# Three-chunk value visits, transposed cluster scores and a re-planned order in a clustered-attention and mixture kernel

## The chip, the cores and the metric

The kernel runs on one core of a Trainium2 chip, as one launch. The metric is the device time of a launch in microseconds. The core has five engines that run their own instruction queues in order: TensorE (PE in the profile; its weight loads PEld), VectorE (DVE), ScalarE (ACT), GpSimd (POOL) and SyncE (SP), whose queue issues most transfers. Results of TensorE land in PSUM; everything else lives in SBUF.

## The reference

Sixteen heads of attention (2 batches x 8 heads, 768 positions, head size 64) in which a query sees only the keys whose nearest centroid is its own, then a soft mixture of eight experts with four slots each, then a gated layer. Cut to what matters:

```python
q_assign = argmax(einsum('bhsd,hcd->bhsc', q_n, c_n))   # 16 clusters
k_assign = argmax(einsum('bhsd,hcd->bhsc', k_n, c_n))
scores = where(q_assign == k_assign, scale * q @ k.T, -1e9)
attn = softmax(scores) @ v
x = attn.transpose(0, 2, 1, 3).reshape(B * S, H * D)
logits = x @ phi                                        # 8 experts x 4 slots
slot_input = softmax(logits, axis=0).T @ x
slot_out[e] = relu(slot_input[e] @ w1[e]) @ w2[e]
x = softmax(logits, axis=1) @ slot_out
xn = x / sqrt(mean(x * x) + 1e-6) * rms_g
out = (silu(xn @ w_gate) * (xn @ w_val)) @ w_out
```

## The kernel before

Heads are taken two at a time: eight pairs, numbered i. `prepare(i)` loads q, k and v of a pair, splits every value into a high and a low part (`tokq`, `tokk`; the low part is a subtraction on GpSimd or VectorE), turns the result with TensorE (`ptk`, `ptq`, L331) and copies it out of PSUM (`k1`, `q1`). It does so in two halves g of 384 positions. Per half it then forms the centroid scores of q and k (`pc`, L368), copies them to SBUF (`cs`), brings them back to one position per partition by products against a constant `G2` that adds the two partial sums (`sc`, L378), finds the winning cluster with five VectorE steps (`am`, `E`, L399 to L408) and turns the one-hot rows `E` with TensorE (`pe`, L419). ScalarE writes them into the extra rows of `q2` and `k2` (`oq`, `ok`), so that the score products also carry the mask.

A unit u is one half of the queries of a pair: 16 units. Each first computes raw scores (`s1`, L489) whose row maxima VectorE takes (`nm`, L501), turns the maxima (`pm`, L519) and moves them into a row of `q2` with a transfer (`mrow`). Then six key chunks c follow: the scores again, with mask and maximum (`s2`, L541 and L543, four passes), the exponential on ScalarE (`P`, L550), the sum of the P tiles on GpSimd (`acc`, L217) and the value products (`o`, L567), which use 64 of the 128 columns of the array, one head in each half. `AVN = 2` makes one visit to the value products for every two chunks, so three visits per unit. `RINGS` gives the number of buffers of each kind; P has `PR = 5`, and PSUM gives three buffers to `big` (s1, s2, transposes, row sums) and one each to `ms` (`pc`, `sc`, `pe`, `pm`, `po`) and `av` (`o`).

Nothing of the order is written out by hand. Every step is an `op` with its possible engines and their estimated durations, its inputs, the buffers that it takes and a key, the time at which it is due in units; `KO` shifts the key of a kind of step. `Sched.run` lists the steps one after the other: it takes the one that could start first by the estimates, plus a penalty for a later key (`WK`), and thereby fixes each engine's queue.

The weights of the last layer arrive as 64-bit words and are decoded beside attention: 24 tiles into `wgv`, two into `wo4`, each with a step on ScalarE (`mag`) and two on VectorE (`bits`, L914 and L916). The experts' weights, 64 loads of 512 KB, go into 31 places that are freed one after another (`xa` to `xc`, `rawk` to `tokq`, rings `w0`, `wx`, `wz`, `wv`, `wy`); the last four rings open when parts of the attention buffers are closed. After attention come the slot sums (`middle`), the experts (`h1`, `h2`), and the gated layer in three groups of tokens (`g`, `v`, `hf`, `hh`, `hl`, `o`, L1614).

Of the kernel before, what the change touches and what calls it, by code (L numbers as in the profile page):

```python
# [7 lines left out]
F32 = mybir.dt.float32  # L8
# [9 lines left out]
C = 16  # L18
# [9 lines left out]
def bc(ap, n):  # L28
# [16 lines left out]
WK = 6.8
# [13 lines left out]
DK = 1.74  # L59
# [7 lines left out]
PT = 219.23  # L67
# [44 lines left out]
class Sched:  # L112
# [7 lines left out]
    LAT = dict(pe=200, act=150, dve=130, pool=80)  # L120
# [21 lines left out]
    def run(self):  # L142
# [9 lines left out]
        done = 0  # L152
        while avail:
            best = None
            k0 = min(o.key for o in avail)
            for o in avail:
# [24 lines left out]
            free[e] = st + busy  # L181
            o.end = st + dur
# [41 lines left out]
class Attention:  # L224
# [7 lines left out]
    def __init__(self, tc, sched, K, q, k, v, X, pools, cw):  # L232
# [7 lines left out]
        self.lastE = []  # L240
        self.final = {}
# [35 lines left out]
    def prepare(self, i):  # L277
# [22 lines left out]
        def half(g):  # L300
# [44 lines left out]
            for n, nm in enumerate("kq"):  # L345
# [5 lines left out]
                l = op({"pool": (1020, 1020, 0 if i else P0), "dve": 550}, split_lo(nm), key=zg - 14.5, uses=[(a, t), (O[r], r)])  # L351
                p = op({"pe": 550}, trans(nm), key=zg - 12 + 0.4 * n, alloc=("big", nm + "1", nm + "2"),
# [1470 lines left out]
```

## Time and profile before

| | |
|---|---|
| median of 3 runs | 500.8 us (500.64 to 501.13) |
| the profiled execution | 499.88 us, of which the span of the trace 497.8 us |
| TensorE busy | 467.3 us (94%), 2872 instructions |
| VectorE, ScalarE, GpSimd busy | 318.1 us, 283.8 us, 191.2 us |
| read from HBM | 61.97 MB |

The profile gives the busy time of every engine, the time of every instruction and what it waited for. The stages stand one after another in the span: opening to 30 us, attention to 297.4, slot sums to 310, experts to 361, the start of the gated layer to 376.4, its products to 491.5 and the last output to 497.8. A busy time is that of the whole stretch asked for; the granted clock is TensorE's, 1.00 for 2.4 GHz.

### The profile page before, as it was taken

Reading aid. Unit: us, or ns where it says so; the run is one execution under the profiler, and the core shown is the slowest. Engines: PE = TensorE matmul, PEld = TensorE weight load, DVE = VectorE, ACT = ScalarE, POOL = GpSimd, SP = SyncE. Lnnn points to the kernel's source line nnn. Section 1 sums busy time; section 2 is a strip of 40 time slices with the busy share of each in tenths; the row PEclk is TensorE's granted clock in tenths of the full one; section 3 lists DMA queues with packets and bytes.
Section 4 is the critical chain, followed back from the end, with each engine's and each line's share of the span. In section 5 each row is a group of like instructions: output and inputs, shape, how many; then the busy total and the mean of one; then the engine's idle time right before and its main releaser. Section 6 shows DMA issues by size and latency. Waiting matters only on the chain.

```text
span 497.8 us, 7957 instructions
## 1 busy us (share of the span) xinstructions
PE 467.3 (94%) x2872; PEld 328.1 (66%) x2872; DVE 318.1 (64%) x607; ACT 283.8 (57%) x586; POOL 191.2 (38%) x130
## 2 busy tenths in 40 slices
PE   7899998999999999999999997989899999999996
PEld 6766676675766856765765774335347888888884
DVE  6879998989999999765738236100169884443430
ACT  5687686696795876865551653220248665335331
POOL 2237745666574656655464650100214550000000
PEclk9999999999999999999998998999999999999999
DMA  6564633634634541203922974899922302002002
GB/s 182 155 197 116 197 122 95 169 113 124 182 114 110 172 133 48 65 17 105 349 91 85 348 257 158 343 390 403 394 78 86 127 1 84 2 0 86 0 0 84
DMA packets 30822, 71.96 MB, mean 145 GB/s; under 512 B 4064, under 2 KB 10304, under 8 KB 30784
## 3 DMA queue, kind: packets, MB, share of 16 engines
q1 hardware_dynamic: 26080, 55.73, 33.3%
q10 hardware_dynamic: 4704, 15.73, 10.1%
q8 instruction: 22, 0.36, 0.3%
q14 instruction: 16, 0.13, 0.1%
HBM read 61.97 MB, written 3.15 MB: 131 GB/s over the span
## 4 chain that ended last, share of the span: by engine, by line
PE 73%; DVE 14%; DMA 6%; ACT 3%; issue 2%; ACTq 0%; POOL 0%; SPq 0%; DVEq 0%
PE o L1614 20%; PE o L567 11%; PE s L541 8%; PE s L543 6%; DVE nm L501 5%; PE s L489 5%; DMA w<-in_moe_w_dram 4%; PE h L1297 2%; PE pc L368 2%; DVE wgv L916 2%; PE h L1271 2%; PE g L1578 2%; PE v L1578 2%; PE pl L598 2%; PE sc L378 1%
## 5 line engine op out<-in xcount | busy, mean ns | idle before, releaser
L217 POOL TENSOR_TENSOR acc<-acc,P 128x768 f32<-128x768 f32 x62 | 115.3, 1860 | 49.5 <-ACT P L550 47.2
L550 ACT ACTIVATE P<-s 128x768 f32<-128x768 f32 x96 | 76.1, 812 | 45.7 <-PE s L543 43.8
L501 DVE TENSOR_REDUCE nm<-s 128x1 f32<-128x768 f32 x96 | 88.5, 950 | 19.6 <-PE s L489 18.7
L1614 PE MATMUL o<-W,hh 128*128 128x512 f32 x288 | 89.6, 392 | 0.0
L541 PE MATMUL s<-q,k 128*128 128x384 f32 x192 | 72.2, 376 | 3.4 <-DVE nm L501 2.8
L567 PE MATMUL o<-P,rawv 128*64 128x384 f32 x384 | 72.1, 498 | 0.0
L543 PE MATMUL s<-q,k 97*128 97x384 f32 x192 | 65.4, 341 | 0.9 <-DMA q<-nr 0.9
L1614 PEld LDWEIGHTS o<-W,hh 128*128 128x128 f32 x288 | 53.9, 188 | 12.2
L1614 PE MATMUL o<-W,hl 128*128 128x512 f32 x144 | 56.7, 394 | 0.0
L489 PE MATMUL s<-k,q 96*128 96x384 f32 x192 | 51.7, 370 | 1.4 <-DVE nm L501 1.3
L217 POOL TENSOR_TENSOR acc<-P,P 128x768 f32<-128x768 f32 x16 | 29.6, 1849 | 56.2 <-ACT P L550 56.2
L541 PEld LDWEIGHTS s<-q,k 128*128 128x128 f32 x192 | 36.5, 190 | 18.7 <-DVE nm L501 8.3
L1590 DVE TENSOR_TENSOR hf<-v,sg 128x512 f32<-128x512 f32 x36 | 24.6, 689 | 33.6 <-PE v L1578 30.1
L567 PEld LDWEIGHTS o<-P,rawv 128*64 128x64 f32 x384 | 23.5, 136 | 28.1 <-issue 26.8
L489 PEld LDWEIGHTS s<-k,q 96*128 96x128 f32 x192 | 32.0, 193 | 11.8 <-DVE nm L501 5.5
L543 PEld LDWEIGHTS s<-q,k 97*128 97x128 f32 x192 | 36.8, 192 | 1.2 <-DMA q<-nr 1.2
L217 POOL TENSOR_TENSOR W<-wo,W 128x512 fp32r<-128x512 f32 x10 | 13.9, 1389 | 58.8 <-DMA w<-in_moe_w_dram 35.9
L1586 ACT ACTIVATE sg<-g 128x512 f32<-128x512 f32 x36 | 21.3, 598 | 24.9 <-PE g L1578 24.7
L209 ACT CAST hh<-hf 128x512 fp32r<-128x512 f32 x34 | 21.1, 621 | 22.1 <-PE o L1614 21.0
L217 DVE TENSOR_TENSOR hl<-hf,hh 128x512 fp32r<-128x512 f32 x32 | 24.5, 766 | 13.0 <-ACT hh L209 12.3
L1614 PEld LDWEIGHTS o<-W,hl 128*128 128x128 f32 x144 | 27.0, 188 | 6.1
L623 ACT ACTIVATE pl<-pl 128x128 f32<-128x128 f32 x84 | 22.0, 262 | 8.3 <-PE pl L605 4.6
(250 smaller groups left out, 740.0 us busy)
## 6 DMA issues: line engine op xcount, KB each, us to landing
w<-in_moe_w_dram SPq DMA_DIRECT2D x56, 512.0 KB, 7.3
gate<-in_moe_w_gate_dram ACTq DMA_DIRECT2D x12, 512.0 KB, 3.5
val<-in_moe_w_val_dram ACTq DMA_DIRECT2D x12, 512.0 KB
out<-in_moe_w_out_dram SPq DMA_DIRECT2D x10, 512.0 KB, 4.9
rawk<-in_k_dram SPq DMA_DIRECT2D x8, 384.0 KB, 3.6
rawq<-in_q_dram SPq DMA_DIRECT2D x8, 384.0 KB, 3.8
rawv<-in_v_dram SPq DMA_DIRECT2D x8, 384.0 KB, 4.7
k<-k SPq DMA_DIRECT2D x16, 192.0 KB, 3.1
```

The source lines that it names most:

```text
L209: nc.scalar.copy(out, in_)
L217: (nc.vector if e == "dve" else nc.gpsimd).tensor_tensor(out, a, b, op=op)
L489: nc.tensor.matmul(ps[:, g, :HQ], T[q2][0:96, h, qb : qb + 128], T[f"k2_{i}_{g}"][0:96, h, :], start=True, stop=True,)
L501: nc.vector.tensor_reduce(T[f"nm{u}"][:, n : n + 1], T[f"s1_{u}{h}{j}"][:, :, :HQ], op=ALU.max, axis=AX.XY, negate=True)
L541: nc.tensor.matmul(ps[:, h, :HQ], T[f"k1_{i}_{g}"][:, h, kb], T[q1][:, h, :], start=True, stop=False)
L543: nc.tensor.matmul(ps[:, h, :HQ], T[f"k2_{i}_{g}"][0:97, h, kb], T[q2][0:97, h, :], start=False, stop=True)
L550: nc.scalar.activation(p, T[f"s2_{u}_{c}"][:, :, :HQ], AF.Exp, scale=float(1.0 / D**0.5))
L567: nc.tensor.matmul(T[f"o{u}"][64 * h : 64 * h + 64, :HQ], T[f"rawv{i}"][:, h, c, :], T[f"P{u}_{c}"][:, h, :], start=(c == 0), stop=(c == N ...
L623: nc.scalar.activation(p, p, AF.Copy, accum_out=ls_()[:, h, j : j + 1])
L1586: nc.scalar.activation(self.tile(f"sg{tg}_{f}", [128, 512], F32, "sg", "outp", 2), T[f"g{tg}_{f}"], AF.Silu)
L1590: nc.vector.tensor_tensor(self.tile(f"hf{tg}_{f}", [128, 512], F32, "hf", "outp", 2), T[f"v{tg}_{f}"], T[f"sg{tg}_{f}"], op=ALU.mult)
L1614: nc.tensor.matmul(T[f"o{tg}{q}"], T[f"{x}{tg}_{f}"][:, ts], T[f"W{f // 6}"][:, w, f % 6, :], start=(f == 0 and n == 0), stop=(f == 11 and ...
```

## The change

The value products are made in two visits of three chunks (`AVN = 3`), and P has seven buffers. The cluster scores are turned by three transposes against the identity instead of products with `G2`; the two partial sums that the product added are added by a new VectorE step `part` with two reductions. The one-hot rows of q and k lie side by side in a tile 96 wide, so that three transposes bring all of them (`E` is written in another layout, and `oq` and `ok` read the new place); the constants `escale` and `ebias` move with them, and `G2` goes. The planner charges TensorE for going into and out of the value products and for starting after a gap, has other durations, other delays between engines, two new order constraints (`lastT`) and new numbers in its tables. The ring `wx` has six places instead of eight, `wv` and `wy` five instead of four each.

```diff
-PR = 5
+PR = 7
-AVN = 2
+AVN = 3
-NW0, NWX, NWZ, NWV, NW1 = 4, 8, 4, 4, 4
+NW0, NWX, NWZ, NWV, NW1 = 4, 6, 4, 5, 5
...
 KO = {
-    "oT": -6.7, "s1": 0.19, "lT": -0.03, "split_hi": 17.5, "osb": -15.77, "mag": 8.64, "guard": 7.48, "argmax": -16.77,
+    "oT": -7.28, "s1": -0.53, "lT": 1.63, "split_hi": 87.73, "osb": -14.23, "mag": 11.6, "guard": 7.48,
+    "argmax": -7.55, "oevac": 15.28, "clusterT": 3.91, "lsum": 0.75, "onehot": -2.04, "acc": -35.81, "av": 33.0,
...
-    LAT = dict(pe=200, act=150, dve=130, pool=80)
+    LAT = dict(pe=180, act=140, dve=100, pool=80)
+
+    HALF = ("av",)
+    TO, FRO, COLD = 140, 200, 100
...
+        def more(o, e, st):
+            if e != "pe" or o.key > 99:
+                return 0
+            h = opname(o.fn) in self.HALF
+            return (self.TO if h else self.FRO) if h != half else 0 if h or st < free.get(e, 0.0) + 5 else self.COLD
+
...
-                l = op({"pool": (1020, 1020, 0 if i else P0), "dve": 550}, split_lo(nm), key=zg - 14.5, uses=[(a, t), (O[r], r)])
+                l = op({"pool": (1250, 1250, 0 if i else P0), "dve": (850, 850, SLP if i else 0)}, split_lo(nm), key=zg - 14.5, uses=[(a, t), (O[r], r)])
...
                 for j in range(3):
-                    nc.tensor.matmul(pt[:, 64 * j : 64 * j + 64], T[f"cs{i}{g}"][:, j * 128 : (j + 1) * 128], K["G2"],
-                                     start=True, stop=True)
+                    at = slice(j * 128, (j + 1) * 128)
+                    nc.tensor.transpose(pt[:, 128 + j * 128 :][:, :128], T[f"cs{i}{g}"][:, at], K["id"])
+
+
+            def part(e):
+                pt = T[f"sc{i}{g}"]
+                for a, b in ((0, 128), (128, 192)):
+                    nc.vector.tensor_reduce(pt[:, a:b].rearrange("p (m c) -> p m c", c=C),
+                                            pt[:, 128 + 2 * a : 128 + 2 * b].rearrange("p (m t c) -> p m c t", t=2, c=C),
+                                            op=ALU.add, axis=AX.X)
...
+            self.lastT = [p]
+            p = op({"dve": 640}, part, key=zg - 9.9, uses=[SC])
...
-                            self.tile("E", [128, 3, 65], BF16, "E")
-                            nc.vector.memset(T["E"][:, :, 64:], 1.0)
+                            self.tile("E", [128, 3, 96], BF16, "E")
+                            nc.vector.memset(T["E"][:, :, 32:64], 1.0)
...
                 pt = self.bank(f"pe{i}{g}", ms).bitcast(BF16)
-                for n in range(2):
-                    for j in range(3):
-                        at = n * HQ + j * 128
-                        nc.tensor.transpose(pt[64:97, at : at + 128], T["E"][:, j, 32 * n : 32 * n + 33], K["idb"])
+                for j in range(3):
+                    nc.tensor.transpose(pt[:96, j * 128 : (j + 1) * 128], T["E"][:, j], K["idb"])
...
-                pv.append(op({"pe": 650 * AVN + 170}, av(cs), key=zu + c + 1.3, alloc=() if pv else ("av",),
+                pv.append(op({"pe": 646 * AVN + 10}, av(cs), key=zu + c + 1.3, alloc=() if pv else ("av",),
```

Three places in the queues show what the tables do. TensorE, in the middle of attention: units 6 (`o6`, `s2_6`) and 7, the second half of pair 4 (`sc41`, `pe41`); "..." stands for the second head's two passes of the same score step. Before:

```order
L378 MATMUL sc41_1726<-G2_132,cs41_1682 128x64 x3
L598 MATMUL pl5_1735<-idr_102,acc5_1519 128x128 x6
L605 MATMUL pl5_1735<-phi_99,os5_1671 128x64 x3
L541 MATMUL s2_6_3_1751<-q1_3_0_1034,k1_3_1_1238 128x384
L543 MATMUL s2_6_3_1751<-q2_3_0_1035,k2_3_1_1239 128x384
...
L567 MATMUL o6_1764<-P6_0_1689,rawv3_1304 64x384 x2
L567 MATMUL o6_1764<-P6_1_1724,rawv3_1304 64x384 x2
L419 LDWEIGHTS E_296
L419 MATMUL pe41_1776<-idb_104,E_296 33x128
```

And now, the same place:

```order
L403 MATMUL sc41_1721<-idr_102,cs41_1692 128x128 x3
L355 MATMUL ptq50_1735<-idr_102,tokq5_0_1588 128x128 x6
L601 MATMUL o6_1745<-P6_0_1612,rawv3_1280 64x384 x2
L601 MATMUL o6_1745<-P6_1_1651,rawv3_1280 64x384 x2
L601 MATMUL o6_1745<-P6_2_1676,rawv3_1280 64x384 x2
L575 MATMUL s2_7_0_1767<-q1_3_1_1159,k1_3_0_1053 128x384
L577 MATMUL s2_7_0_1767<-q2_3_1_1160,k2_3_0_1054 128x384
...
L453 LDWEIGHTS E_302
L453 MATMUL pe41_1776<-idb_104,E_302 96x128
```

The visit takes three chunks, and the row sums of unit 5 (`pl5`) have moved ahead of `sc41`. VectorE at the same place, the steps that make the one-hot rows (`wgv` is a weight decode, `nr7` and `l5` belong to units 7 and 5). Before:

```order
L501 TENSOR_REDUCE nm7_1599<-s1_712_1712 128x1
L916 SCALAR_TENSOR_TENSOR wgv_151<-val1_3_1454,daval1_3_1616 128x512
L399 TENSOR_REDUCE am41_1745<-sc41_1726 128x12
L401 TENSOR_TENSOR sc41_1726<-sc41_1726,am41_1745 128x192
L404 SCALAR_TENSOR_TENSOR sc41_1726<-sc41_1726,iota_113 128x192
L406 TENSOR_REDUCE am41_1745<-sc41_1726 128x12
L408 TENSOR_TENSOR E_296<-sc41_1726,am41_1745 128x3x64
```

And now:

```order
L945 SCALAR_TENSOR_TENSOR wgv_150<-gate1_1_1416,dagate1_1_1674 128x512
L409 TENSOR_REDUCE sc41_1721<-sc41_1721 128x128
L409 TENSOR_REDUCE sc41_1721<-sc41_1721 128x64
L433 TENSOR_REDUCE am41_1752<-sc41_1721 128x12
L435 TENSOR_TENSOR sc41_1721<-sc41_1721,am41_1752 128x192
L668 TENSOR_SCALAR pl5_1706<-pl5_1706 128x6
L438 SCALAR_TENSOR_TENSOR sc41_1721<-sc41_1721,iota_113 128x192
L670 RECIPROCAL l5_1758<-pl5_1706 128x6
L440 TENSOR_REDUCE am41_1752<-sc41_1721 128x12
L442 TENSOR_TENSOR E_302<-sc41_1721,am41_1752 128x3x2x32
```

The two reductions come in, two small steps of unit 5 stand between, and the decode ahead is an earlier one (`gate1_1` for `val1_3`): decodes now run to unit 14, where they ended in unit 10. SyncE near the end of attention: `nr13` to `nr15` are the maxima of the last units, the `w` loads are expert weights. Before:

```order
L204 DMA q2_6_1_2427<-nr13_2940 1x6x128
L204 DMA q2_7_0_2595<-nr14_3103 1x6x128
L880 DMA w21_2_3128<-in_moe_w2_dram 128x2x512
L880 DMA w20_1_3143<-in_moe_w2_dram 128x2x512
L880 DMA w20_3_3153<-in_moe_w2_dram 128x2x512
L880 DMA w21_1_3165<-in_moe_w2_dram 128x2x512
L880 DMA w21_3_3189<-in_moe_w2_dram 128x2x512
L880 DMA w12_0_3205<-in_moe_w1_dram 128x1024
L204 DMA q2_7_1_2797<-nr15_3191 1x6x128
L880 DMA w13_0_3215<-in_moe_w1_dram 128x1024
```

And now:

```order
L227 DMA q2_6_1_2357<-nr13_2891 1x6x128
L227 DMA q2_7_0_2543<-nr14_3057 1x6x128
L227 DMA q2_7_1_2746<-nr15_3169 1x6x128
L909 DMA w21_2_3187<-in_moe_w2_dram 128x2x512
L909 DMA w20_1_3208<-in_moe_w2_dram 128x2x512
```

The six loads that stood ahead of unit 15's maxima stand behind them.

## Rows read from the trace of the kernel before

**Rows 1.** Busy times by stretch: us; PE, PEld, DVE, ACT, POOL; clock, DMA share, GB/s
```profile
30.00:297.40 267.40, 255.78 (x1565) 179.66 (x1564) 209.07 (x379) 184.37 (x401) 157.16 (x89) 0.99 0.46 145
88.00:192.10 104.10, 100.41 (x625) 71.31 (x625) 95.93 (x171) 79.26 (x179) 63.55 (x36) 1.00 0.46 134
268.40:272.40 4.00, 4.00 (x15) 3.33 (x14) 2.86 (x4) 1.12 (x3) 2.65 (x2) 0.57 0.35 131
297.40:310.00 12.60, 8.92 (x85) 6.03 (x82) 6.80 (x25) 4.96 (x20) 0.00 (x0) 0.86 0.55 198
310.00:361.00 51.00, 47.47 (x417) 19.87 (x417) 5.55 (x17) 10.42 (x20) 4.39 (x10) 1.00 0.98 374
376.40:491.50 115.10, 115.10 (x506) 93.80 (x505) 63.01 (x86) 56.88 (x99) 17.39 (x12) 1.00 0.12 42
```

**Rows 2.** TensorE's waits in attention (us, times, longest), and one in time
```profile
PE s L541 <- DVE nm L501: 2.8, 7, 0.7
PE pc L368 <- DVE k L211: 2.5, 4, 0.7
...
264.85 0.62 PE L489 MATMUL s<-k,q 96*128 96x384 f32 x2 [0.34 <-DVE nm L501]
```

**Rows 3.** TensorE in time (start, us): around one value visit, and a double one
```profile
142.02 0.34 PE L541 MATMUL s<-q,k 128*128 128x384 f32 x1
142.20 0.34 PE L543 MATMUL s<-q,k 97*128 97x384 f32 x1
142.46 1.51 PE L567 MATMUL o<-P,rawv 128*64 128x384 f32 x8
143.90 0.44 PE L541 MATMUL s<-q,k 128*128 128x384 f32 x1
144.18 0.34 PE L543 MATMUL s<-q,k 97*128 97x384 f32 x1
...
292.91 2.80 PE L567 MATMUL o<-P,rawv 128*64 128x384 f32 x16
```

**Rows 4.** TensorE in time: one-hot rows, three transposes, cluster scores, with followers
```profile
134.10 0.51 PE L419 MATMUL pe<-idb,E 128*33 128x128 bf16 x6
134.54 0.62 PE L489 MATMUL s<-k,q 96*128 96x384 f32 x2
...
160.46 0.55 PE L628 MATMUL po<-idr,os 128*128 128x128 f32 x3
160.76 0.42 PE L541 MATMUL s<-q,k 128*128 128x384 f32 x1
...
161.91 0.78 PE L378 MATMUL sc<-G,cs 128*128 128x64 f32 x6
162.50 0.59 PE L489 MATMUL s<-k,q 96*128 96x384 f32 x2
```

**Rows 5.** VectorE's groups, 88 to 192.1 us (the last: whole run): busy us, mean ns
```profile
L501 DVE TENSOR_REDUCE nm<-s 128x1 f32<-128x768 f32 x36 | 33.5, 951 | 4.8 <-PE s L489 4.4
L916 DVE SCALAR_TENSOR_TENSOR wgv<-gate,dagate 128x512 int32<-128x512 int32 x8 | 10.4, 1298 | 0.0
L914 DVE TENSOR_SCALAR dagate<-dagate 128x512 int32<-128x512 int32 x8 | 9.9, 1251 | 0.0
L211 DVE CAST k<-ptk 128x768 fp32r<-128x768 f32 x4 | 3.8, 944 | 0.0
L217 DVE TENSOR_TENSOR tokq<-rawq,tokq 128x384 fp32r<-128x384 f32 x3 | 3.4, 1141 | 0.0
L401 DVE TENSOR_TENSOR sc<-sc,am 128x192 f32<-128x192 f32 x6 | 2.2, 361 | 0.3
...
L673 DVE TENSOR_REDUCE L<-pl 128x64 f32<-128x128 f32 x4 | 1.1, 284 | 0.1
```

**Rows 6.** SyncE's queue in time (start, us)
```profile
269.73 3.01 SPq L880 DMA_DIRECT2D w<-in_moe_w_dram  x6
...
279.27 63.62 SPq L880 DMA_DIRECT2D w<-in_moe_w_dram  x43
```

More of the change, by code (lines that the diff above doesn't have):

```diff
@@ L30, in bc @@
     return ap.unsqueeze(len(ap.shape)).to_broadcast(list(ap.shape) + [n])
-SH = 8.49
-SH1 = 2.63
+SH = 9.28
+SH1 = 2.66
 DMAT = 2400.0
 DMAB = 600.0
-SHP = 11.22
-SHQ = 2.9
+SHP = 20.84
+SHQ = 1.84
 SLK = 2000.0
 NKQ = 4
-DG = 2.05
-LP = 753.69
-DP = 301.31
-PR = 5
-WK = 6.8
+DG = 3.0
+LP = 18052.37
+DP = 232.12
+PR = 7
+WK = 7.76
 WKT = 200.0
@@ L66 @@
 WC = 500.0
-PT = 219.23
+WM = 0.3
+SLP = 477.95
+PT = 478.56
 OA = 2
@@ new lines @@
+LGP = 61.14
+AVN = 3
+LP = 18052.37
+AP = 13381.6
+GP = 6842.73
+XP = 9896.11
+NW0, NWX, NWZ, NWV, NW1 = 4, 6, 4, 5, 5
+KO = {
+    "oT": -7.28, "s1": -0.53, "lT": 1.63, "split_hi": 87.73, "osb": -14.23, "mag": 11.6, "guard": 7.48,
+    "argmax": -7.55, "oevac": 15.28, "clusterT": 3.91, "lsum": 0.75, "onehot": -2.04, "acc": -35.81, "av": 33.0,
+    "evac": 0.88, "bits": -1.18, "nmT": -13.35, "split_lo": -42.25, "s1max": -8.76, "cevac": 5.66, "nrow": 21.47,
+    "cluster": 2.34, "csum": -9.29, "lga": -22.47, "lgm": 69.26, "hh": 58.86, "pre": -0.68, "rms0": -0.9, "h2e": -6.42,
+    "part": -3.71, "low": -39.37, "soh": 0.05, "hl": 17.17, "gh": -6.79, "cTe": -49.34, "raw": -10.52, "om": 1.29,
+    "cT": -3.78, "sot": -2.04, "lo": 43.74, "gcols": -64.55, "put4": 26.77, "x2s": -1.21, "gp": 51.24, "hi": 9.62,
+    "silu": -18.04, "x2": -66.93, "rows": 0.57, "siT": -12.69, "si": -40.13, "dz": 3.33, "mx": -17.5, "mp": 28.55,
+    "dexp": 52.02, "sie": -25.75, "cq": -18.95, "qhi": -20.63, "fexp": -29.39, "gram": 0.46, "socs": -103.61,
+    "fold": 23.44, "fsi": 46.62, "fz": -35.81, "qlo": -7.16, "drec": -53.26, "mv": -38.65, "linv": -26.33,
+    "xrow": -11.36, "exp": 6.89, "trans": -1.86, "mrow": -23.15, "oq": -16.8, "sums": 3.0, "tok": 8.0, "ok": 10.96,
+    "centroids_": 25.86, "cols": -11.58, "csm": -43.42, "ds": 5.45, "dsum": -45.11, "fes": -34.61, "four": 0.49,
+    "h1": 87.53, "h2": -3.34, "hT": -9.72, "hTe": 8.9, "hf": 47.46, "high": -17.99, "lgt": 24.63, "lgx": -82.97,
+    "lgx0": 21.44, "load": 65.08, "mb": 42.7, "mm": -0.66, "mp1": -28.22, "mpT": 3.01, "od": -42.59, "oe": 10.74,
+    "put": -3.64, "relu": 62.21, "rms": -79.22, "root": 30.84, "s2": -1.24, "scale": -8.08, "sel": 42.33,
+    "setup": -61.3, "siT0": 6.25, "siTe": 5.35, "side": 44.61, "siz": -5.05, "square": -4.15, "to_out": -53.23,
+    "to_tail": 48.79, "to_wp": -24.39, "to_wv": -26.44, "to_wx": 13.35, "to_wz": 14.8, "warm": 19.04, "wload": -10.88,
@@ L152, in run @@
         done = 0
+        half = False
+        def more(o, e, st):
[3 more added lines that the diff above has]
+            return (self.TO if h else self.FRO) if h != half else 0 if h or st < free.get(e, 0.0) + 5 else self.COLD
         while avail:
@@ L173, in run @@
                     pen = d[2] if isinstance(d, tuple) and len(d) > 2 else 0
+                    pen += WM * more(o, e, st)
                     pen += min((WK if o.key < 99 else WKT) * (o.key - k0), WC)
@@ L180, in run @@
             busy, dur = d[:2] if isinstance(d, tuple) else (d, d)
-            free[e] = st + busy
-            o.end = st + dur
+            x = more(o, e, st)
+            if e == "pe" and o.key <= 99:
+                half = opname(o.fn) in self.HALF
+            free[e] = st + busy + x
+            o.end = st + dur + x
             o.seen = o.end + self.LAT.get(e, 0)
@@ L509, in unit @@
                 key = zu - 5.5 + 0.66 * n - sh
-                p = op({"pe": 420}, s1(h, j), key=key,
+                p = op({"pe": 360}, s1(h, j), key=key,
                        deps=O["q2r", half] + O["k2r", 0] + O["k2r", 1] + ([U[0]] if n else []),
@@ L574, in unit @@
             d = md + O["q2r", half] + O["k2r", c // 3]
-            s = op({"pe": 760}, s2(c), key=zu + c, deps=d, alloc=("big",),
+            s = op({"pe": 715}, s2(c), key=zu + c, deps=d, alloc=("big",),
                    uses=[K1[c // 3], K2[c // 3], Q1, Q2])
@@ L920, in decode @@
         a = op({"act": (670, 670, pen)}, mag, key=key, deps=deps, after=[self.prev[0]], uses=[src], alloc=("da",))
-        b = op({"dve": (600, 600, pen)}, bits(0), key=key + 0.01, uses=[(a, "da")])
-        d = op({"dve": (1050, 1050, pen)}, bits(1), key=key + 0.02, deps=[b], after=[self.prev[1]], alloc=alloc,
+        b = op({"dve": (920, 920, pen)}, bits(0), key=key + 0.01, uses=[(a, "da")])
+        d = op({"dve": (1270, 1270, pen)}, bits(1), key=key + 0.02, deps=[b], after=[self.prev[1]], alloc=alloc,
                uses=[src, (a, "da")])
```

53 lines of the change are left out of this document (21 added, 32 removed), and 3 rows, old and new, of the table KO.

## The prediction

> **What bounds the kernel now.** I cut the span into stages first [rows 1] and asked of each who ends it. In the attention stretch from 30 to 297.4 us TensorE is busy for 255.78 of 267.4 us, VectorE for 209.07, so TensorE sets the pace with 11.6 us of gaps. In the three steady pairs of units from 88 to 192.1 us (34.7 us each) the two stand closer together: TensorE 100.41, VectorE 95.93 of 104.1, which is 92% for VectorE. From 310 to 361 us, the experts, the DMA share is 0.98: this stage ends when the last expert weight has landed, whatever TensorE could do. From 376.4 to 491.5 us TensorE has no gap at all, and the change takes no multiplication out of that stage. The end of the attention stretch is therefore what can move, and the later stages follow it as a block if the experts' transfers keep their distance to it.
>
> Next I read what TensorE waits for inside the stretch [rows 2]. The largest two are the row maxima (`nm`, L501) and the copy of the transposed keys out of PSUM (`k`, L211), both on VectorE; 2.5 us hang on the latter, in four waits. To the gaps comes a slow piece: from 268.4 to 272.4 us TensorE is busy throughout at a mean granted clock of 0.57, so mostly at 1.2, the lower of the two levels (2.4 GHz is the other), after score products (`s1`) that had waited one by one for a maximum [rows 2]. At full clock that work takes 4.0 x 0.57 = 2.3 us, so 1.7 us are lost. Gaps and clock together are 13.3 us, the most that a better order could give back in attention.
>
> **The value products, 46 visits to 30.** A visit to the half-width products (`o`, L567) costs more than its passes. In [rows 3] the last score pass starts at 142.20, the second one after the visit at 144.18; passes of the scores start 0.18 us apart, so the visit occupies 144.00 - 142.38 = 1.62 us. Its eight passes are worth 1.29 us: that is the difference between the entry with 16 passes (2.80) and the one with eight (1.51). The remaining 0.33 us is paid per visit, for going in, draining and coming out. The old order has 46 visits (two of the 48 stand back to back with another), the new order 30, counted in the listings. 16 x 0.33 = 5.3 us of TensorE. The bounds are 0, if the cost sits in the passes, and 5.3.
>
> **Cluster scores turned by transposes.** Six passes against `G2` start at 161.91 and the next work at 162.50, 0.59 us [rows 4]. Three transposes of the same kind of data (`po`, L628) take from 160.46 to 160.76, 0.30 us, and the work behind either starts up alike. I take 0.30 for the new step, so 0.29 x 16 = 4.6 us; if each new transpose cost as much as two old passes, nothing would be gained, so the bounds are 0 and 4.6.
>
> **One transpose for the one-hot rows.** Six products took 134.10 to 134.54 = 0.44 us [rows 4]. Half as many, 96 columns wide instead of 33, should take 0.22; the bounds are 0.22 and 0.44, since nothing in the trace shows that width here. I take 0.22, because the row is for the same 128 columns that pass in each; 0.22 x 16 = 3.5 us. The three parts together are 13.4 us of TensorE, 1.7 us per pair.
>
> **What VectorE pays.** The two cluster hypotheses now are added by two reductions per half, of 256 and of 128 values per partition. The nearest rows are a reduction of 128 values, 284 ns, and of 768 values, 951 ns [rows 5]: in between, 256 values take about 0.42 us, so 0.70 us per half and 1.4 per pair. Against that, in a steady pair: the `k` copy leaves VectorE (0.94 us), both subtractions for `tokq` and `tokk` leave it in most pairs (1.14 for the one in the row; I count 1.7 for both), and the 26 weight decodes, about five per pair in this stretch (eight of its 15 are in the row), are spread over units 2 to 14, some four per pair: one less, 1.30 + 1.25 = 2.6 us. The pair needs 95.93/3 = 32.0 + 1.4 - 0.9 - 1.7 - 2.6 = 28.2 us of VectorE, 87% of a pair of 32.6 us (34.7 less 1.7 and a part of the stalls). So the reductions cost nothing as long as VectorE keeps that room. Without the cover, in the opening before 30 us, the chain from scores to one-hot rows is exposed twice; there the sum is 2 x 0.70 - 2 x (0.29 + 0.22) = 0.4 us; I charge 0.3 because one of the old constants goes, bounds 0 and 1.
>
> **What ScalarE, GpSimd and the queues pay.** ScalarE gets about one key copy more per pair, 0.94 us at VectorE's price [rows 5] beside 79.26/3 = 26.4 of 34.7 us [rows 1], and two row sums in the whole program; it has 8 us of room per pair. GpSimd gets nine more subtractions over the program; at VectorE's 1.14 us [rows 5] that is 1.3 us per pair, and it was busy for 63.55/3 = 21.2 us of a pair. In the last stage seven subtractions go from VectorE to GpSimd and four casts from ScalarE to VectorE; TensorE without a gap hides them, and if it did not, each would cost at most its own length. Seven P buffers instead of five let exponentials run ahead of a visit of three chunks, which is what makes the longer visit harmless. On SyncE the maxima of unit 15 now go ahead of all the late expert loads, where six loads stood ahead of them. In the old trace those six were issued at 269.73, the rest from 279.27 on [rows 6]; now all 20 loads that depend on the freed attention buffers (6 + 4 + 5 + 5) begin behind that row. At the pace of the experts' stage, 51 us at 374 GB/s [rows 1], a load of 0.524 MB takes 1.4 us, so 20 take 28 us. Behind the product that feeds that row stand eight score steps of 0.72 us (four passes), four three-chunk visits of 2.3 us and the last row sums, some 18 us of TensorE work to the end of attention, and 12.6 us of the middle stage follow before the first expert product: 30.6 us. The loads fit by 2.6 us. If that cover were gone, each load that is late delays the experts by 1.4 us; bounds 0 and 7 (five loads), and I take 0.
>
> **Where the stalls go.** The wait for the `k` copy (2.5 us) should go, since ScalarE makes the copy and, between the transpose and its reader, TensorE now has a visit of 2.3 us and four `s1` steps to do. The slow piece (1.7 us) should go, because the maxima of unit 14 are no longer computed in one run of six but between score products and value visits. I count these two, 4.2 us; the bounds are 0 and 13.3.
>
> **The sum.** The profiled execution took 499.9 us (497.8 of span, 2.1 around it). 499.9 - 13.4 + 0.3 - 4.2 = 482.6; the median of the three timed runs is 0.9 above the profiled one, which gives 483.5 us. With no stall removed it is 487.7.
>
> **Rivals.** (1) VectorE sets the pace in part. Each one-hot product now waits for seven VectorE steps instead of five. On TensorE the transposes of one half and its one-hot product are separated by 0.5 + 0.97 x 2 + 0.33 + 0.72 = 3.5 us of work in the new order; VectorE needs 0.70 + 5 x 0.36 [rows 5] and two small steps, some 2.9 us, and a decode of 1.30 us stands ahead. A mean wait of 0.5 us per half costs 8 us: 491.5.
>
> The Trainium skill, SBUF — State Buffer, "Who interferes with whom", says that an instruction of GpSimd and certain ones of VectorE lock each other out of a shared port for a whole instruction; nine more subtractions on GpSimd speak for this rival by that rule. The decode steps' means of 1.25 and 1.30 us in the shared stretch agree with such blocking, though the trace does not name its cause.
>
> (2) Slower: the same wait, but at every half and as long as a decode. The place is the one-hot product on TensorE, in whose queue everything behind it stands, the scores of the next unit first. It turns the gain into a loss from (13.4 + 4.2 - 0.3)/16 = 1.1 us of mean wait on; at 1.30 + 0.4 = 1.7 us it gives 483.5 + 27 = 511. For it speaks that VectorE is first in, first out; against it that the decodes now are 4 per pair and only one stands ahead of a half.
>
> (3) The visits don't cost what I read. If the 0.33 us sits with the passes, 5.3 us stay: 489.
>
> (4) The clock. The slow piece came after waits, yet it could come from what TensorE does too. If each of the 16 new transposed steps brought a piece as in [rows 1], with 1.7 us lost, the time would be 483.5 + 27 = 511 as well. The steady pairs hold over 40 fp32 transposes each at a granted clock of 1.00 [rows 1], which speaks against it.
>
> This is where the Trainium skill speaks against the change: TensorE: Matmul & The Clock Gate, "Part 4: PE-mode transpose", says that transposes don't count as activity for the clock. By that rule alone the time would be rival 4's; this trace's stretch at 1.00 bears it out only a little.
>
> **How the numbers follow.** Forecast 0.66 (478 to 488), rival 1 0.16, rival 3 0.08, rival 2 0.05, rival 4 0.02, and 0.03 for more stalls gone than I count (below 478). The range 478 to 491.5 holds the forecast, rival 3 and half of rival 1: 0.82. Faster by more than 0.2% (1.0 us, what a measurement of this kernel can tell from no change): 0.91; within 0.2%: 0.02, from rival 1 at its worst; slower: 0.07, rivals 2 and 4.
>
> **What would show it.** Right: a steady pair of about 32.6 us instead of 34.7; 30 visits of which one with twelve passes takes about 2.1 us; `sc` at 0.3 us and `pe` at 0.2; attention ending near 281 us and the experts' stage still about 51 us long. Wrong: TensorE idle ahead of `pe` with VectorE as releaser (rivals 1, 2), clock below 1.00 in the steady pairs (4), an experts' stage that is longer because loads start late, or a tail that is no longer gapless.

## The result and the profile after

The changed kernel takes 497.31 us in the median (five runs, 494.29 to 498.85), the kernel before 500.8: a ratio of 0.990, 95% interval 0.986 to 0.994. It is faster by 1%, where 483.5 us and at most 491.5 were forecast. The direction was right; four fifths of the gain are missing. Ratios here and below leave out executions that took over 1.5% more than the fastest of the same kernel.

The profiled execution took 497.95 us. Its page, busy times and granted clock in 40 slices of 12.4 us (9 is 90% or more):

```profile
span 496.2 us, 7824 instructions
PE 462.4 (93%) x2776; PEld 329.2 (66%) x2776; DVE 320.3 (65%) x631; ACT 280.9 (57%) x601; POOL 211.2 (43%) x144
PEclk9978979999999998999999989999979999999999
```

TensorE was busy for 467.3 us before, for 462.4 now, 4.9 less, though 13.4 us of work were to go. The row of the clock has the reason: 7s and 8s, in six slices. The listing of every execution gives the span with its mean granted clock, so the time that the clock took can be worked out for each: (1 - clock) x span. It is 0.007 x 497.8 = 3.5 us in the profiled execution of before and 0.031 x 496.2 = 15.4 us in this one. Of the 13.8 us by which the program itself grew shorter, **11.9 went to TensorE at half clock.**

Three stretches, cut at the row of maxima of unit 2 (`pm`) and at that of unit 15, show where. Columns as in [rows 1]; the three lines of before, then the three of after:

```profile
0.00:46.80 46.80, 40.51 (x304) 31.55 (x304) 36.68 (x91) 30.92 (x50) 18.12 (x19) 1.00 0.62 170
46.80:277.80 231.00, 220.44 (x1358) 156.23 (x1358) 188.77 (x337) 158.59 (x345) 133.02 (x75) 0.99 0.42 129
277.80:497.80 220.00, 206.39 (x1213) 140.35 (x1212) 92.62 (x180) 94.25 (x192) 40.02 (x37) 0.99 0.42 155
```

```profile
0.00:51.50 51.50, 42.61 (x280) 32.50 (x280) 39.16 (x100) 28.19 (x45) 17.36 (x19) 0.90 0.52 147
51.50:272.90 221.40, 208.30 (x1278) 153.82 (x1278) 184.69 (x350) 162.47 (x371) 143.67 (x84) 0.98 0.42 124
272.90:496.20 223.30, 211.45 (x1221) 142.90 (x1218) 96.45 (x182) 90.27 (x186) 50.18 (x42) 0.98 0.45 165
```

The 13 units in the middle take 221.4 us instead of 231.0, with the clock at 0.98. The first stretch is 4.7 us longer, at a clock of 0.90, which is a loss of 5.2; the last is 3.3 us longer. Four slow stretches themselves, in which TensorE has half its clock most of the time:

```profile
30.00:36.00 6.00, 6.00 (x23) 5.08 (x23) 4.33 (x6) 4.11 (x6) 1.00 (x1) 0.57 0.44 106
44.00:50.00 6.00, 5.41 (x20) 2.55 (x21) 3.56 (x5) 0.60 (x2) 3.14 (x2) 0.72 0.21 66
68.00:76.00 8.00, 6.87 (x22) 6.53 (x23) 3.31 (x6) 4.01 (x7) 3.65 (x2) 0.58 0.17 59
186.00:194.00 8.00, 6.56 (x34) 3.42 (x36) 6.03 (x9) 2.53 (x5) 3.63 (x3) 0.79 0.28 76
```

The first begins at 28 us. They cost 1.7 us (44, 188) or 3.4 us (28, 69), where the one piece in [rows 1] cost 1.7; two more stand at 294 to 298 and 359 to 366. What TensorE did ahead of them is in its waits (us in total, times, longest) and, for three of them, in time:

```profile
PE po L662 <- ACT k L462: 4.7, 6, 1.7
PE s L523 <- DVE nm L535: 3.5, 6, 1.2
PE pe L453 <- DVE E L442: 3.0, 5, 1.2
PE pl L639 <- ACT pl L657: 2.2, 1, 2.2
PE fmb L1007 <- DVE fmx L1004: 1.4, 1, 1.4
```

```profile
44.59 0.62 PE L523 MATMUL s<-k,q 96*128 96x384 f32 x2 [1.20 <-DVE nm L535]
...
66.33 0.51 ACT L232 CAST tokk<-rawk 128x384 fp32r<-128x384 f32 x1 [3.13 <-DMA rawk<-in_k_dram]
...
68.95 0.65 PE L662 MATMUL po<-idr,os 128*128 128x128 f32 x3 [1.74 <-ACT k L462]
...
188.89 0.63 PE L1007 MATMUL fmb<-idr,fmx 32*128 32x32 f32 x2 [1.38 <-DVE fmx L1004]
```

In [rows 2] no wait is longer than 0.7 us, but the rows are not all of them. The longest two of the kernel before in attention, the opening aside, stand at 76 and 226.5 us, with the clock at 1.00 behind both:

```profile
PE ptq L331 <- DVE nm L501: 1.3, 2, 1.1
PE fmb L978 <- DVE fmx L975: 1.1, 1, 1.1
```

Now `po` waits 1.74 us, because ScalarE stood for 3.13 us at a copy (`tokk3_0`) whose load was late, with the writes `k2_2_0` behind it, which hold the PSUM bank that `po` needs; `s1_210` waits 1.20 us for a maximum, and `fmb`, a product that spreads the largest logit so far, 1.38 us for a copy on VectorE. TensorE's clock is at half soon after each, and so it is behind the 2.20 us that `pl` waits at 294. The stretch at 359 is another case: no wait right ahead of it is longer than 0.35 us.

The parts themselves read as forecast: `sc`, `ptq` behind it, a visit of twelve passes with its follower, and a `pe`:

```profile
64.77 0.37 PE L453 MATMUL pe<-idb,E 128*96 128x128 bf16 x3
64.94 0.96 PE L523 MATMUL s<-k,q 96*128 96x384 f32 x4
...
176.36 0.50 PE L403 MATMUL sc<-idr,cs 128*128 128x128 f32 x3
176.62 0.71 PE L355 MATMUL ptq<-idr,tokq 128*128 128x128 f32 x6
177.26 2.16 PE L601 MATMUL o<-P,rawv 128*64 128x384 f32 x12
179.34 0.44 PE L575 MATMUL s<-q,k 128*128 128x384 f32 x1
```

`sc` takes 0.26 us (0.30 forecast), `pe` 0.17 (0.22), the visit 2.08 (2.1). VectorE's two reductions are 0.425 and 0.300 us in its groups, 0.73 a half (0.70 forecast):

```profile
L409 DVE TENSOR_REDUCE sc<-sc 128x128 f32<-128x256 f32 x16 | 6.8, 425 | 4.8 <-PE sc L403 3.1 <-issue 1.7
L409 DVE TENSOR_REDUCE sc<-sc 128x64 f32<-128x128 f32 x16 | 4.8, 300 | 0.6
```

### The profile page after: what moved, and what is told of

The parts are those of the page before. It is cut to its first block, busy times and chain, and to the rows that moved or that the text cites. A ratio compares the mean times of both kernels' runs of the same rounds, so it can differ in the third digit from the quotient of the medians.

```text
span 496.2 us, 7824 instructions
## 1 busy us (share of the span) xinstructions
PE 462.4 (93%) x2776; PEld 329.2 (66%) x2776; DVE 320.3 (65%) x631; ACT 280.9 (57%) x601; POOL 211.2 (43%) x144
## 4 chain that ended last, share of the span: by engine, by line
PE 65%; DVE 15%; ACT 8%; DMA 6%; issue 5%; POOL 0%; ACTq 0%; DVEq 0%; POOLq 0%
PE o L1643 19%; PE o L601 9%; PE s L523 5%; PE s L575 4%; DMA w<-in_moe_w_dram 4%; PE s L577 4%; DVE nm L535 4%; PE h L1326 2%; PE h L1300 2%; ACT pl L657 2%; DVE wgv L945 2%; PE v L1607 2%; PE g L1607 1%; PE ptk L355 1%; PE pc L392 1%
## 5 line engine op out<-in xcount | busy, mean ns | idle before, releaser
L240 POOL TENSOR_TENSOR acc<-acc,P 128x768 f32<-128x768 f32 x62 | 118.1, 1904 | 33.2 <-ACT P L584 29.4
L575 PE MATMUL s<-q,k 128*128 128x384 f32 x192 | 70.0, 365 | 1.7 <-DVE nm L535 1.1
L523 PE MATMUL s<-k,q 96*128 96x384 f32 x192 | 53.7, 380 | 4.5 <-DVE nm L535 3.5
L601 PEld LDWEIGHTS o<-P,rawv 128*64 128x64 f32 x384 | 25.7, 141 | 30.3 <-issue 29.2
L232 ACT CAST hh<-hf 128x512 fp32r<-128x512 f32 x30 | 18.6, 622 | 34.4 <-PE o L1643 34.4
L240 POOL TENSOR_TENSOR hl<-hf,hh 128x512 fp32r<-128x512 f32 x11 | 17.1, 1556 | 46.1 <-PE o L1643 42.2
L240 DVE TENSOR_TENSOR hl<-hf,hh 128x512 fp32r<-128x512 f32 x25 | 18.3, 732 | 21.5 <-ACT hh L232 14.9
```

The costliest lines, as they stand in the source:

```text
L232: nc.scalar.copy(out, in_)
L240: (nc.vector if e == "dve" else nc.gpsimd).tensor_tensor(out, a, b, op=op)
L523: nc.tensor.matmul(ps[:, g, :HQ], T[q2][0:96, h, qb : qb + 128], T[f"k2_{i}_{g}"][0:96, h, :], start=True, stop=True,)
L575: nc.tensor.matmul(ps[:, h, :HQ], T[f"k1_{i}_{g}"][:, h, kb], T[q1][:, h, :], start=True, stop=False)
L601: nc.tensor.matmul(T[f"o{u}"][64 * h : 64 * h + 64, :HQ], T[f"rawv{i}"][:, h, c, :], T[f"P{u}_{c}"][:, h, :], start=(c == 0), stop=(c == N ...
```

## Experiments

Theory 1: TensorE's longer waits in the new order bring the half clock, and that is where the gain went. Theory 2: the transposes bring it. Theory 3: it was waits for other engines, and the clock is beside the point. "At equal clock" below is a run's time less (1 - clock) x span, as a median over the runs of a kernel; it is 496 to 497 for the kernel before in every comparison, and for the changed one 482.6 and, timed again on another chip (e13_empty), 481.3. It is a rough measure: a straight line through the executions of the kernel before gives about 0.7 us of time for each us of this loss, not 1. Differences of one or two us between experiments of different chips say little.

**Fill the waits (e1_fill).** A table names six `s1` steps behind which idle matmuls stand, written into columns of the same bank that nobody reads:

```diff
+FILL = {6: 8, 7: 15, 8: 5, 14: 20, 21: 24, 63: 20}
...
+                for _ in range(FILL.get(6 * u + 3 * h + j, 0)):
+                    nc.tensor.matmul(ps[:, 0, HQ:], K["idb"], K["idb"], start=True, stop=True)
```

> The changed kernel with its order untouched; at six places where its TensorE waits (three in the run of s1 of unit 1 around 26 to 30 us, the 1.20 us ahead of s1_210 at 44.6, the 1.74 us ahead of po at 68.9, the 1.38 us ahead of fmb at 188.9) between 5 and 24 idle matmuls of 128 columns (0.06 us each by the warm rows) follow the s1 that stands ahead of the wait and write columns of its bank that nobody reads. Theory 1 (each of these waits is followed by a stretch in which TensorE is granted half its clock, and that is where the gain went): the stretches at 28.3-35.9, 45.3-48.6, 69.3-76 and 188.1-192.9 run at 1.00, which gives back about 3.6+1.8+3.4+2.2 = 11 us: 486 to 489 us, although no wait is gone. Theory 2 (the transposes that took the place of the products bring the lower clock): the stretches stay, 497 to 499 us. Theory 3 (the time went to waits for VectorE and ScalarE, not to the clock): 497 to 499 us, too, with the clock back or not.

Measured: 488.96 us, ratio 0.975 (0.969 to 0.982), clock 0.985 to 0.995 in its four runs; the changed kernel's five have 0.968 to 0.975. The four slow stretches of above are at 1.00 in its profile, where one of 1.7 us at 350 to 354 is left, and the three sections become:

```profile
30.00:36.00 6.00, 5.13 (x25) 3.62 (x24) 5.28 (x9) 4.81 (x8) 1.00 (x1) 1.00 0.52 146
44.00:50.00 6.00, 6.00 (x32) 3.85 (x33) 5.26 (x8) 2.11 (x4) 2.38 (x2) 1.00 0.22 66
68.00:76.00 8.00, 8.00 (x59) 7.03 (x60) 5.71 (x14) 6.66 (x19) 7.32 (x5) 1.00 0.12 27
186.00:194.00 8.00, 7.77 (x57) 6.19 (x50) 5.68 (x8) 4.40 (x9) 4.05 (x3) 1.00 0.67 200
...
0.00:49.10 49.10, 41.38 (x330) 32.00 (x330) 39.58 (x100) 28.25 (x45) 17.35 (x19) 1.00 0.54 154
49.10:265.10 216.00, 205.97 (x1321) 152.75 (x1322) 184.94 (x350) 162.40 (x371) 143.58 (x84) 1.00 0.43 127
265.10:485.20 220.10, 207.30 (x1221) 140.43 (x1218) 96.37 (x182) 90.22 (x186) 50.33 (x42) 0.99 0.45 168
```

Work that computes nothing made the kernel 8 us faster than the changed kernel of the first comparison, 6 us faster than the same kernel in e13_empty (494.66), and its slowest execution (490.29) is ahead of the fastest of all nine of those (491.69). So the loss of clock is what took the gain, and it hangs on what TensorE does at these places: no transpose went, and theories 2 and 3 asked for no change. That each wait brings its own stretch is not shown by it: `pl` still waits 2.20 us at 286 us, and there the clock stays at 1.00. By its median it is the fastest version of this study.

**Take the waits away (e2_moves).** Four places in the queues change: ScalarE's `tokk3_0` goes behind the last `k2_2_0`; TensorE's second visit of unit 0 goes ahead of `s1_210`, a visit of unit 9 ahead of `fmb`, `gram` behind the first `gp` (these two and `cq` are products at the start of the gated layer).

> The changed kernel with four instructions or visits in another place of their engine's order and nothing else: on ScalarE the copy tokk3_0 (which waits 3.13 us at 66.3 for its load) behind q2_2_0 and the two k2_2_0; on TensorE the second visit of unit 0 ahead of s1_210, the visit of unit 9 ahead of fmb, gram behind the first gp. Theory 1: waits of 1.74, 1.20 and 1.38 us ahead of po, s1_210 and fmb go, and with them the half-clock stretches behind them (1.8+3.4+2.2 us) and the one at 359-366 (3.4 us): 483 to 487 us. Theory 2: the clock stays as it is and only idle time of some 4 us goes: 492 to 494 us. Theory 3: the waits come back at the next instruction that needs the same engine: 495 to 498 us.

Measured: 492.01 us, ratio 0.983 (0.976 to 0.990), clock 0.976 to 0.981. Of the slow stretches those at 44, 68 and 186 us are gone from its profile; the opening's (28 to 36) stays, as meant, with a new one at 14 to 20, and those at 290 to 296 and 352 to 360 stay too: `gram` moved, but a wait of 0.80 us came up ahead of `cq`. At equal clock it is 482.7, the changed kernel's own 482.6 or 481.3: the idle time that I took away at three places came back at others, as theory 3 has it. Whether the moves gave anything is open: the four executions (491.73 to 495.11 us) lie among those of e13_empty, the changed kernel without them (491.69 to 495.65), whose profile lacks the stretches at 44 and 68 us too.

**Moves and opening together (e6_all, e9_more).** e6_all has the moves, `cq` behind the second `gp` as well, and the opening's three fills. e9_more adds fills at the two stretches left:

```diff
+                for _ in range(36):
+                    nc.tensor.matmul(pt[:, 1, HQ + 72 :], K["idb"], K["idb"][:, :56], start=True, stop=True)
...
+                for _ in range(24 if ep == 3 else 0):
+                    nc.tensor.matmul(ps[:, 128:256], K["idb"], K["idb"], start=True, stop=True)
```

> The changed kernel with the moves of e2_moves, the idle matmuls of e1_fill in the opening alone (behind three s1 of unit 1), and cq moved behind the second gp as well, so that gram, gp and cq stand as in the kernel before. Theory 1: the stretches at half clock that are left in e2_moves at 28-36 (3.4 us) and 352-360 (3.4 us) go, so 492.0 less 6 to 7 us: 485 to 487 us; the fills ahead of po, s1_210 and fmb were worth no more than the moves that took those waits away. Theory 3 (only the order in the loop of pairs counts): 490 to 492 us.

> e6_all with idle matmuls in the two stretches where its clock still falls: 36 of 56 columns behind the transposes pl of unit 15 (TensorE waits 2.20 us there for the sums that ScalarE makes) and 24 of 128 columns behind the last sc of the experts (waits of 0.29 to 0.61 us around gp, gram and cq). Theory 1: the stretches at 286-294 (3.4 us) and 350-362 (5.1 us) run at 1.00: 484 to 487 us. If the clock falls there for another reason than TensorE's waits: 491 to 494 us.

Measured: e6_all 492.14 us, ratio 0.980 (0.976 to 0.985); e9_more 490.5, ratio 0.979 (0.973 to 0.984). Both miss theory 1's range (up to 487 us). In e6_all's profile the opening is clean, but 286 to 294 and 350 to 362 us are slow, so the order of `gram`, `gp` and `cq` is not what set the clock there. In e9_more the second is clean; the first, at 290 to 296, is still slow behind its fill, and one stands at 14 to 20. The stretch at 350 in e6_all:

```profile
350.00:362.00 12.00, 12.00 (x52) 5.44 (x48) 4.71 (x15) 3.64 (x7) 1.78 (x2) 0.57 0.14 46
```

and in e9_more, first the stretch, then TensorE in time:

```profile
350.00:362.00 12.00, 10.44 (x76) 4.71 (x73) 6.47 (x19) 5.09 (x10) 1.79 (x2) 1.00 0.16 53
```

```profile
349.15 1.50 PE L1400 MATMUL sc<-idb 128*128 128x128 bf16 x24
351.26 1.08 PE L1553 MATMUL gp<-wgv,SOg 128*64 128x512 f32 x4 [0.61 <-DVE SOg L1405]
```

But the reader of `sc` on VectorE now starts behind the fill, since the fill writes the tile that it reads: `gp` still waits 0.61 us, 1.5 us later, and the clock behind this wait is now 1.00. At equal clock e9_more is 487.0 against e6_all's 484.4, on two chips. These fills bought clock with time of about the same size.

**One fill, and none (e12_one, e13_empty).** The fill ahead of `po` alone, and the changed kernel with an empty table.

> The changed kernel with one of e1_fill's six fills alone: 24 idle matmuls behind s1_311 (the last s1 ahead of the 1.74 us wait of po for k2_2_0). Theory 1: the stretch at 69-76 runs at 1.00, those at 28-36, 45-49 and 188-193 stay at half: 3.4 us less than the changed kernel of this call, 493 to 495 us if that one takes 497. If the clock were a state of the whole run and not set wait by wait: all stretches back, or none.

> The changed kernel itself (the table of fills is empty), timed beside e12_one on one chip: 494 to 499 us, the half-clock stretches at 28-36, 45-49, 69-76, 188-193 and 359-366 in the profile as in the first one, if they are set by the program's own waits.

Measured: 494.32 and 494.66 us; no difference. The expectation of e13_empty fell in part, and with it the test: its profile has no slow stretch at 44 and 68 us, though one at 14 to 20 that the first profile lacks. Three of its stretches, and two of its waits:

```profile
44.00:50.00 6.00, 4.77 (x25) 2.77 (x25) 5.26 (x7) 1.64 (x4) 3.85 (x3) 1.00 0.22 66
68.00:76.00 8.00, 7.95 (x54) 7.81 (x55) 5.88 (x13) 6.17 (x16) 7.41 (x5) 1.00 0.15 47
186.00:194.00 8.00, 8.00 (x41) 4.43 (x38) 4.48 (x10) 3.29 (x6) 0.88 (x1) 0.82 0.50 173
```

```profile
45.36 0.61 PE L526 MATMUL s<-k,q 96*128 96x384 f32 x2 [1.23 <-DVE nm L540]
...
67.22 0.55 PE L667 MATMUL po<-idr,os 128*128 128x128 f32 x3 [0.99 <-ACT k L465]
```

`s1_210` waits 1.23 us here, as in the first profile, and this time the clock holds; `po` waits 0.99 us, since the load came sooner. So one such wait does not fix what follows, and what one fill is worth stays open. The sum does come out alike: the nine executions of the changed program have clocks of 0.968 to 0.978, the kernel before 0.976 to 0.997 in the 54 that were timed beside the experiments.

**Put waits into the kernel before (e5_gaps).** At the third `s2` of units 4, 8 and 12, one, two and three reductions on VectorE that TensorE has to wait for:

```diff
+GAP = {(4, 2): 1, (8, 2): 2, (12, 2): 3}
...
+                if (u, c) in GAP:
+                    nc.tensor.matmul(ps[:, 0, HQ:], K["idb"], K["idb"], start=True, stop=True)
+                    for _ in range(GAP[u, c]):
+                        nc.vector.tensor_reduce(ps[:, 0, HQ : HQ + 1], K["CW"][:, :768].bitcast(F32), op=ALU.max, axis=AX.X)
+                    nc.tensor.matmul(ps[:, 0, HQ:], K["idb"], K["idb"], start=True, stop=True)
```

> The kernel before with three waits put into TensorE's order: behind the third s2 of units 4, 8 and 12 TensorE writes 128 columns that nobody reads, VectorE reduces 128x768 elements (0.95 us each by its rows) one, two and three times into the same columns, and TensorE writes them again before it goes on; so TensorE stands still for about 1.3, 2.2 and 3.2 us, and longer where VectorE has something queued. Theory 1: behind each such wait from some length on stands a stretch of several us with the clock granted at half, 1 to 3.5 us lost in each: 509 to 518 us, mean clock 0.98 or lower. Theories 2 and 3: the clock stays at 1.00 behind the waits and the time grows by their sum, some 7 us, or less: 503 to 508 us.

Measured, in one execution: 511.52 us, clock 0.980, which the kernel before has itself at times (0.976 to 0.997). The three waits in time, then the stretches behind them:

```profile
105.45 0.22 PE L552 MATMUL s<-idb 128*128 128x128 bf16 x1 [1.11 <-DVE s L551]
...
177.23 0.22 PE L552 MATMUL s<-idb 128*128 128x128 bf16 x1 [2.11 <-DVE s L551]
...
255.23 0.22 PE L552 MATMUL s<-idb 128*128 128x128 bf16 x1 [3.12 <-DVE s L551]
```

```profile
105.40:112.00 6.60, 6.55 (x47) 4.65 (x48) 5.73 (x16) 5.45 (x17) 4.23 (x3) 1.00 0.15 46
177.20:185.20 8.00, 7.97 (x38) 5.64 (x38) 5.51 (x17) 4.48 (x16) 3.62 (x3) 0.58 0.21 66
255.20:261.00 5.80, 5.77 (x31) 3.69 (x30) 3.27 (x10) 3.63 (x5) 2.84 (x2) 0.71 0.70 255
```

Behind 1.11 us the clock stays; behind 2.11 us it falls and 3.4 us are lost (0.42 x 8.0), behind 3.12 us 1.7. The waits add up to 6.3 us, and the kernel took 11 us more than the 500.6 of its comparison, as theory 1 expected. So slow stretches stand right behind two of three waits in the old program, with none of the change in it. But a third one, 28 to 32 us (1.7 us), stands behind none of the waits put in, and there is only this one execution: what a wait of a given length costs is not shown by it.

**The two transposed parts on the old order (e4_parts, e8_onehot).** The kernel before with its own queues. e4_parts has the new `clusterT`, the two reductions ahead of the first maximum, and the new `onehot`, `E` and `ok`; e8_onehot the last three alone.

> The kernel before, order, numbers and visits untouched, with two parts of the change alone: the cluster scores turned by three transposes and added up by two reductions on VectorE (0.73 us more VectorE work a half), and one transpose of 96 rows for three one-hot rows. Theory 1: TensorE saves 16 x (0.29+0.22) = 8.1 us, the clock stays at 0.99 of full speed and no stretch at half clock is new: 492 to 495 us. If VectorE's longer chain ahead of E is waited for at each half, up to 0.7 us a half of it is lost again: 499 to 503 us. Theory 2: stretches at half clock appear behind the transposes, the mean clock falls to 0.97 or less: 503 us or more.

> The kernel before with one part of the change alone, that costs VectorE nothing: one transpose of 96 rows in place of two for the one-hot rows. If TensorE's passes set the time of the kernel before: 16 x 0.22 = 3.5 us less, 496 to 498 us. If in the old order VectorE sets the pace (in e4_parts TensorE waited 1.05 us a pair for nm ahead of ptk, which it did not before), the saved time turns into waits for nm: 499.5 to 501.5 us.

Measured: e4_parts 504.29 us, ratio 1.006 (1.002 to 1.010), slower; e8_onehot 499.95, ratio 0.996 (0.993 to 0.9995). At equal clock 496.7 and 494.0, with 497.0 and 496.1 for the kernel before beside them: the one-hot rows give about 2 of their 3.5 us, and the score transposes take them back. Two pairs (113 to 183 us) in the kernel before:

```profile
113.00:183.00 70.00, 67.60 (x422) 47.85 (x420) 64.58 (x115) 53.44 (x120) 43.02 (x25) 1.00 0.46 136
```

in e4_parts:

```profile
113.00:183.00 70.00, 65.38 (x393) 45.24 (x392) 62.52 (x122) 52.09 (x119) 42.15 (x24) 1.00 0.46 132
```

and the longest of TensorE's waits there in e4_parts:

```profile
PE ptk L331 <- DVE nm L506: 2.1, 2, 1.0
```

TensorE works 2.2 us less and waits 2.1 us for `nm` where it had not: in the old order what TensorE saves turns into waits for VectorE, which is busy for 92% of this window before and 89% in e4_parts. In these windows it is no matter of the clock, which is 1.00 through both, transposes or not. Over the whole run the clock of e4_parts is lower, 0.986 in the median against 0.992 beside it, and its profile has slow stretches at 14 to 20, 28 to 36, 270 to 281 and 308 to 315. The time of theory 2 (503 us or more) was met, but e10_vector below, which adds work on VectorE and no transpose, has a median clock of 0.987 against 0.990, and there the transposes can have no part in it.

**What VectorE's time costs (e10_vector, e11_twice), and the products back (e7_products).** e10_vector is the kernel before with two idle reductions a half (9.6 us in all). e11_twice is e1_fill with each reduction of `part` made twice (11.6 us). e7_products is e1_fill with the six products against `G2` and no reductions.

> The kernel before with more work for VectorE and none less for TensorE: at each of the 16 halves two reductions of 128 columns into 64 (0.30 us each by the changed kernel's row for that form) into columns that nobody reads, ahead of the first maximum of the chain of E: 9.6 us of VectorE in all. If VectorE sets the pace of the old order in the loop of pairs (so that e4_parts lost its saving): 506 to 510 us. If TensorE's passes set it and VectorE's chain has room: 500 to 502 us.

> e1_fill (the changed kernel with its waits filled) with each of the two reductions of the cluster scores made twice, 0.73 us of VectorE more a half, 11.6 us in all, with no change of the result. If VectorE sets the pace there as it does in the old order: 495 to 500 us. If the new order has room on VectorE: within 2 us of e1_fill's 489.0.

> e1_fill with one part of the change undone: the cluster scores come from six products again, as before, and VectorE's two reductions (0.73 us a half) are not there. If TensorE's passes set the time with the clock held up: 16 x 0.29 = 4.6 us more than e1_fill's 489.0, 492 to 494 us. If VectorE's chain ahead of E was what TensorE waited for, its 0.73 us a half come back and the time is that of e1_fill or less: 485 to 489.5 us. If the transposes lowered the clock (theory 2): the same clock of 0.995 here, and no difference.

Measured: e10_vector 504.97 us, ratio 1.008 (1.004 to 1.011); e11_twice 496.23, ratio 0.990 (0.984 to 0.995); e7_products 488.46 and 492.55, ratio 0.976 (0.970 to 0.983), with two more executions of 496.94 and 500.71 us, clock 0.971 to 0.996 in the four. At equal clock e10_vector is 3.6 above its comparison's 496.3, e11_twice 5.2 above e1_fill's 484.1, e7_products 2.5 above it. e11_twice's 496.23 lies in the range for a VectorE that sets the pace (495 to 500), but 2 of its 7.3 us over e1_fill are the clock; the other two fall between their ranges. At equal clock VectorE's time comes through to about 0.4 of its length in either order, neither fully nor not at all; e11_twice and e7_products are set against e1_fill on another chip, so their differences are good to one or two us. In e11_twice TensorE's waits for `E` are 8.4 us where e1_fill has 2.9. So the score transposes seem to be worth 2.5 us in the new order, not 4.6; if the 4.6 are all there on TensorE, the reductions cost some 2 us. Whether it is VectorE's load or the longer chain up to `E` that costs them, these runs don't tell apart.

## Why the prediction was wrong

- **What bounds it** was right in the main: the experts' stage stayed at 51 us with the DMA full, the tail without gaps, and the late loads fit. But attention ended at 295.55 us (297.35 before, 281 forecast), and the slot sums, which the sum left at 12.6 us, took 9.0: where TensorE had waited 3.09 us for `X`, it waits no more. That part of the gain is in no term of the forecast.
- **The three parts of TensorE** (13.4 us) came, and more. The middle stretch went from 231.0 - 1.7 = 229.3 us at equal clock to 216.0 in e1_fill, idle matmuls included, where the clock is 1.00: 13.3 us in 6.5 pairs, 2.0 a pair where 34.7 - 32.6 = 2.1 were forecast, with the `k` wait's share in it. Over the whole span TensorE's busy time less the clock's loss fell from 467.3 - 3.5 = 463.8 to 462.4 - 15.4 = 447.0 us, by 16.8; the ends of products are modelled, so that is an estimate. The whole profiled execution at equal clock gave 13.8 us where 15.6 were forecast (13.4 + 2.5 - 0.3); that they lie so close is in part luck too, since more work went than was counted and more waiting came.
- **Where the stalls go** is the step that failed, twice. I asked where the old waits go and counted 2.5 us of them and the slow piece (1.7 us) as gone, and I put new waits and new slow stretches at nothing without a reason. The wait for the `k` copy and the slow piece of unit 14 did go. But TensorE's idle time over the span grew from 30.5 to 33.8 us, where 2.2 less were forecast (2.5 less, 0.3 more in the opening), and the clock took 11.9 us more than before instead of 1.7 less. The second error, 13.6 us, is most of the 15.4 us by which 482.6 missed the profiled 497.95; against the first, 5.5 us, stand the 3.4 us of work that went beyond the 13.4. The gain was lost to the clock, then, and not to the parts of the change. The new order's longest waits in attention are 1.20, 1.38, 1.74 and 2.20 us, against 1.14 and 1.15 in the old.
- **Rival 4** had the price of a slow piece (1.7 us), but sixteen of them, 27 us, where the clock took 15.4 in all, the wrong cause, and a chance of 0.02. e1_fill keeps all 16 transposed steps at a clock of 0.985 to 0.995, and e7_products without `sc`'s has no better one (0.971 to 0.996). The Trainium skill, TensorE: Matmul & The Clock Gate, "Part 4: PE-mode transpose", says that a transpose doesn't count as busy time in the same way as other products. That rule did not decide here: no run shows a fall that comes with the transposes alone.
- **Rival 1** (VectorE in part) was true in part: the waits of `pe` for `E` are 3.0 us in all, not 8. That the reductions cost nothing, as the sum has it, was too low: twice as many cost 5.2 us at equal clock (e11_twice). In the old order, with more on VectorE, the score part was a loss (e4_parts).
- **The opening** was charged 0.3 us. Up to the maxima of unit 2 the changed kernel takes 51.5 us, 46.4 without the clock's loss, against 46.8 before; the 49.1 of e1_fill have 48 idle matmuls in them.

What stays open: what brings a slow stretch in a given execution. The wait of 1.2 us ahead of `s1_210` is in two profiles of the changed program, and only one of them has a slow stretch behind it; the stretch at 359 us has no long wait ahead of it.

## What to carry to other kernels

Ahead of a re-ordering, list TensorE's longest waits, not only their sum: here a loss of clock took most of a gain of 14 us, and most of it stood behind a few waits of 0.9 to 2.2 us. Where such a wait can't be taken away, matmuls that nobody reads, queued ahead of it, can give the clock back, but not in a tile whose reader is what is waited for: there they delay it by their own length. Compare kernels with the granted clock of each run beside the time: (1 - clock) x span is a first, rough measure of what the clock did and what the program.

## What was not expected of the hardware

- Slow stretches came in losses of about 1.7, 3.4 or, twice, 5.1 us (e4_parts 270 to 281, e6_all 350 to 362).
- In one execution (e5_gaps) a wait of 1.11 us left the clock at 1.00, 3.4 us were lost behind one of 2.11 and 1.7 behind one of 3.12: there the price did not grow with the wait.
- The same program, with the same 1.2 us wait at the same place, had the clock at 0.72 behind it in one execution and at 1.00 in another.
